# Windowed attention ahead of two feed-forward stages: 192 keys instead of 256 for each half of a query tile

## The chip, the cores and the metric

The program runs on one core of one Trainium2 chip. The metric is the device time of one execution in microseconds, taken as the median of several runs. The matrix engine TensorE is PE in the profile (its weight loads are PEld), VectorE is DVE, ScalarE is ACT, GpSimd is POOL, and SyncE is SP, which here issues all transfers between HBM and the on-chip memory SBUF. PE writes its results into PSUM, which is read by DVE and ACT alone.

## The reference

Two batches of 768 tokens pass through an attention of 8 heads of 64, in which a query sees the first n_global = 8 keys and the n_local = 96 latest keys, itself among them. Two feed-forward stages with squared ReLU follow. Inputs and results are float32.

```
scores = scale * q @ k.T
keep = is_global | (0 <= q_pos - k_pos < n_local)
scores = where(keep, scores - slope[h] * dist, -1e9)
a = exp(scores - max(scores)); a = a / (sum(a) + 1e-9)
x = a @ v                                       # (1536, 512)
x = (s * relu(x @ w_in)**2 + b) @ w_out         # 512 -> 2048 -> 512
out = relu(x @ w_in2)**2 @ w_out2
```

## The kernel before

The 1536 tokens make 12 query tiles of 128: tile n is block n // 2 of batch n % 2. Tiles 0 and 1 meet only their own 128 keys. Each of the other ten meets 256 keys in two blocks: its own 128, and the 32 first keys of the sequence with the last 96 of the block before it. The host lays these keys and values side by side, so one transfer per tile brings q and both blocks of k, and another brings both blocks of v (`load`).

The attention of a tile goes in these steps, each a task of a planner:
- `qk`, for one half of the heads (four heads, two pairs): one float32 matmul for each head, 64 rows (a head's features) by 128 columns (the queries), with 256 keys streamed through. The two heads of a pair lie in the upper and the lower 64 partitions, and so in two halves of the array; they write two PSUM buffers. A float32 matmul is two passes in the trace, so a `qk` of four matmuls shows as x8.
- `ttr`, on DVE, adds the bias `ND` (one table for each head, written by `consts` and `slopes` at the start) to the scores, stores the sum in SBUF and takes its extreme. `exp`, on ACT, and `norm`, on any of DVE, ACT and POOL, make the probabilities from it, with `rsum` between them for the reciprocal of the sums.
- `tr`, for one pair of heads, transposes 128 x 512 probabilities by four PE transposes of 128x128 into a PSUM buffer, and `tput`, on ACT or DVE, copies these to SBUF.
- `pv`, for a tile: 16 matmuls, each 128 keys by 64 features of v as the weights with 128 queries streamed through; two heads of a pair write the two halves of the partitions, so two matmuls share the array side by side (x32 in the trace). Weights are loaded anew for every pass.
- `xhi` (ACT) and `xlo` (DVE) split the result into two parts X, which the feed-forward matmuls take.

All of this takes PSUM from one pool of four buffers, `psA`: two for a `qk`, one for a `tr`, one for a `pv`.

The feed-forward stages work in three reduced-precision products for each float32 one. The first four of 16 chunks of the first stage (`h`, line 743, and `y`, line 822, 12 matmuls each with 256 tokens streamed) are run between the attention's tiles; `h` of the first 256 tokens needs tiles 0 and 1 only. When the attention is over, `second` opens more buffers and the remaining chunks follow, by a Strassen-like scheme (line 589 and lines 686 and 692). Their weights come as 64-bit numbers, which DVE and ACT decode.

What stands where on each engine is set by `Plan.run`, a list scheduler that is run when the program is built. `order` gives it each task with engines and costs, a due time, buffers and predecessors; the tables `SHIFT` and `PIN` at line 69 move the due times of named tasks and fix the engine of others. Each engine then runs its own list strictly in that order and waits by semaphores. Until the first `h`, the scheduler fills idle PE time with matmuls on a block of zeros (`warm`, line 375), whose result nobody reads.

Of the kernel before, what the change touches and what calls it, by code (L numbers as in the profile page):

```python
# [8 lines left out]
F32 = mybir.dt.float32  # L9
F32R = mybir.dt.float32r  # L10
I32 = mybir.dt.int32
# [14 lines left out]
HALF = (slice(0, D), slice(D, P))  # L26
NF = 4
# [31 lines left out]
def decoded(a):  # L59
# [9 lines left out]
SHIFT = {('at', 2, 0): 33.9, ('at', 3, 3): -39, ('at', 6, 3): 19.8, ('at', 7, 1): 22.2, ('at', 7, 3): -16.6, ('at',  # L69
    9, 2): 47, ('cadd', 10, 1, 1, 0): -83.9, ('cadd', 14, 1, 1, 0): 138, ('cadd', 16, 0, 0, 1): -56, ('cadd', 18, 0,  # L70
    0, 1): 32.3, ('cadd', 24, 0, 1, 1): -68.8, ('cadd', 28, 0, 1, 1): -48.5, ('cadd', 4, 0, 0, 1): -48.7, ('cadd',
# [21 lines left out]
    1): -12.5, ('norm', 4, 1): 170.3, ('norm', 4, 2): 40.3, ('norm', 5, 0): -22.9, ('norm', 6, 1): -2.8, ('norm', 7,  # L93
# [7 lines left out]
    ('qk', 3, 1): -39.7, ('qk', 8, 1): -104.8, ('relu', 2, 1280): 46.4, ('relu', 2, 256): -80.8, ('relu', 20, 1, 0,  # L101
    1): -45.4, ('relu', 22, 1, 0, 1): 119.7, ('relu', 24, 1, 1, 0): 12.5, ('relu', 4, 0, 1, 0): 2.1, ('rs', 10, 0):
# [1302 lines left out]
```

## Time and profile before

| | before |
|---|---|
| median of 3 runs | 598.61 us (598.4 to 598.61) |
| the profiled execution | 598.59 us |
| its span, first to last instruction | 596.8 us |
| PE busy | 586.8 us, 98% |
| DVE busy | 504.8 us, 85% |
| ACT busy | 363.5 us, 61% |
| POOL busy | 107.4 us, 18% |
| HBM read and written | 51.4 MB, 86 GB/s over the span |

The profiled execution lies within 0.02 us of the median, and 1.8 us of it lie outside the span. Busy time of PE is the union of its matmuls, whose ends are modelled and overlap, so what a stretch of matmuls occupies is read from the start of one group to the start of the next. The profile's chain of what ended last is empty for this execution, so the argument goes by the stretches and by the waits.

### The profile page before, as it was taken

How to read it: one execution, taken by the hardware profiler on the slowest of the kernel's cores; microseconds unless marked ns; L12 is line 12 of the kernel's file. 1: busy time of each engine (PE TensorE's matmuls, PEld its weight loads, DVE VectorE, ACT ScalarE, POOL GpSimd, SP SyncE). 2: the span in 40 equal slices, each digit the busy share in tenths (PEclk: the TensorE clock that was granted, in tenths of full speed). 3: DMA queues.
4: the chain of work that ended last, by engine and by line, in shares of the span. 5: the costliest groups of instructions: out<-in, count | busy, mean ns of one | idle time of the engine just before them, and what ended most of it. 6: DMA issues, size and time to landing. Idle time of an engine off the chain costs nothing.

```text
span 596.8 us, 10149 instructions
## 1 busy us (share of the span) xinstructions
PE 586.8 (98%) x3684; PEld 530.5 (89%) x3684; DVE 504.8 (85%) x1133; ACT 363.5 (61%) x796; POOL 107.4 (18%) x179
## 2 busy tenths in 40 slices
PE   7999999999999999999999999999999999999995
PEld 5788888899999989999999999998898989999894
DVE  7898989799999898999989999899987977874542
ACT  6999987776775646656656664666545544444330
POOL 4443424301100210031000121221120111100000
PEclk8999999999999999999999999999999999999999
DMA  7875631031220332204120311313323122100113
GB/s 278 299 268 173 220 109 36 3 107 36 59 84 2 106 86 91 98 8 156 36 93 2 106 36 36 101 41 110 102 70 107 37 70 63 44 1 1 44 64 110
DMA packets 14889, 52.11 MB, mean 87 GB/s; under 512 B 1904, under 2 KB 2160, under 8 KB 14832
## 3 DMA queue, kind: packets, MB, share of 16 engines
q1 hardware_dynamic: 14832, 51.39, 26.0%
q8 instruction: 31, 0.51, 0.4%
q14 instruction: 26, 0.21, 0.1%
HBM read 48.24 MB, written 3.15 MB: 86 GB/s over the span
## 4 chain that ended last, share of the span: by engine, by line


## 5 line engine op out<-in xcount | busy, mean ns | idle before, releaser
L589 PE MATMUL h<-xh,u 128*128 128x384 f32 x448 | 131.0, 337 | 0.0
L692 PE MATMUL yy<-u,gh 128*128 128x512 f32 x360 | 112.0, 392 | 0.0
L589 PE MATMUL h<-th,u 128*128 128x384 f32 x336 | 99.8, 338 | 0.2 <-DVE u L610 0.2
L686 PE MATMUL yy<-gh,u 128*128 128x512 f32 (+1 forms) x384 | 98.7, 337 | 0.0
L589 PEld LDWEIGHTS h<-xh,u 128*128 128x128 f32 x448 | 82.4, 188 | 1.1
L692 PEld LDWEIGHTS yy<-u,gh 128*128 128x128 f32 x360 | 67.1, 188 | 11.7
L589 PE MATMUL h<-xl,u 128*128 128x384 f32 x224 | 75.4, 337 | 0.0
L686 PEld LDWEIGHTS yy<-gh,u 128*128 128x128 f32 x384 | 67.2, 189 | 7.7
L692 PE MATMUL yy<-u,gl 128*128 128x512 f32 x180 | 70.4, 391 | 0.0
L272 ACT ACTIVATE u<-st 128x512 fp32r<-128x512 f32 (+1 forms) x63 | 40.1, 639 | 44.5 <-DVE st L55 18.7
L686 PE MATMUL yy<-gl,u 128*128 128x512 f32 (+1 forms) x192 | 64.8, 338 | 0.0
L589 PEld LDWEIGHTS h<-th,u 128*128 128x128 f32 x336 | 62.0, 188 | 2.3 <-DVE u L610 1.1
L589 PE MATMUL h<-tl,u 128*128 128x384 f32 x168 | 56.5, 337 | 0.0
L272 ACT ACTIVATE st<-st 128x512 f32<-128x512 f32 x64 | 42.8, 678 | 9.8 <-DMA st<-in_moe_w_out_dram 5.7
L52 DVE SCALAR_TENSOR_TENSOR st<-st 128x512 int32<-128x512 int32 x64 | 45.2, 707 | 2.5
L426 ACT ACTIVATE sn<-sn,nm 128x256 f32<-128x256 f32 (+1 forms) x96 | 46.2, 487 | 1.3 <-DVE nm L418 1.1
L55 DVE SCALAR_TENSOR_TENSOR st<-st 128x512 int32<-128x512 int32 x64 | 45.3, 711 | 1.1
L276 POOL TENSOR_SCALAR sn<-sn,rs 128x256 f32<-128x256 f32 (+1 forms) x68 | 34.8, 527 | 50.0 <-DVE rs L432 18.4
L589 PEld LDWEIGHTS h<-xl,u 128*128 128x128 f32 x224 | 42.1, 188 | 1.0
L610 DVE TENSOR_TENSOR u<-h,m 128x384 f32<-128x384 f32 x56 | 30.9, 552 | 14.1 <-PE h L589 13.4
L276 POOL TENSOR_SCALAR u<-st 128x512 fp32r<-128x512 f32 (+1 forms) x29 | 20.6, 712 | 111.6 <-DVE st L55 42.7
L692 PEld LDWEIGHTS yy<-u,gl 128*128 128x128 f32 x180 | 33.8, 188 | 7.5
(146 smaller groups left out, 1224.6 us busy)
## 6 DMA issues: line engine op xcount, KB each, us to landing
st<-in_moe_w_in_dram SPq DMA_DIRECT2D x32, 512.0 KB, 4.3
st<-in_moe_w_out_dram SPq DMA_DIRECT2D x32, 512.0 KB, 3.6
q<-in_qk_dram SPq DMA_DIRECT2D x10, 768.0 KB, 6.1
v<-in_v_dram SPq DMA_DIRECT2D x10, 512.0 KB, 4.8
out_dram<-acc SPq DMA_DIRECT2D x11, 256.0 KB, 2.2
q<-in_qk_dram SPq DMA_DIRECT2D x2, 512.0 KB, 5.6
v<-in_v_dram SPq DMA_DIRECT2D x2, 256.0 KB, 6.7
out_dram<-acc SPq DMA_DIRECT2D x2, 128.0 KB, 3.2
```

Of the source, the lines that this page charges most:

```text
L52: nc.vector.scalar_tensor_tensor(out=lo, in0=hi, scalar=3, in1=lo, op0=ALU.logical_shift_left, op1=ALU.bitwise_or)
L55: nc.vector.scalar_tensor_tensor(out=lo, in0=hi, scalar=-(1 << 31), in1=lo, op0=ALU.bitwise_and, op1=ALU.bitwise_or)
L272: nc.scalar.activation(out=out, in_=in_, func=AF.Copy, scale=scale)
L276: nc.gpsimd.tensor_scalar(out=out, in0=in_, scalar1=scale, scalar2=0.0, op0=ALU.mult, op1=ALU.add)
L426: self.nc.scalar.activation(out=sn[:, x], in_=sn[:, x], func=AF.Exp, scale=-1.0, bias=self.nm[:, n, h:h + 1], accum_out=self.rs[:, n, h:h ...
L589: self.nc.tensor.matmul(ps, p, q, start=first and kt == 0 and x == 0, stop=kt == 1 and x == 2, skip_group_check=not first)
L610: self.nc.vector.tensor_tensor(out=t, in0=self.T["h", a, tp, 1], in1=self.T["m1", a, tp], op=ALU.add)
L686: self.nc.tensor.matmul(yj, p[:, js], q[:, lo:hi], start=first and x == 0 and not (side and j % 2), stop=last and x == 2 and not (side and ...
L692: self.nc.tensor.matmul(y[m], p[:, ms], q, start=first and x == 0, stop=last and x == 2)
```

## The change

For the ten tiles with two key blocks, the 128 queries are taken in two halves of 64, and each half meets 192 keys: a query is at most 96 keys behind its block's start, so the first half needs the far 96, the first 32 and the first 64 of its own, the second half the last 32 of the far ones, the first 32 and all 128 of its own. The parts:

1. `qk`: eight matmuls of 64 rows by 64 columns with 192 keys streamed, where four of 64 by 128 with 256 stood. The four of a head pair lie in the four 64x64 pieces of the array. Score buffer u holds one head for the first 64 queries and the other head for the second 64 (heads swapped between halves); the two matmuls that share an output half write different buffers.
2. `ttr`, `exp`, `norm` and `tput` work on 192 or 384 elements instead of 256 or 512. The bias tables have 192 columns and swap heads too: `consts` has two more iotas on POOL and five more instructions on DVE, and `slopes` scales by a column of exponents instead of a constant.
3. `tr`: three transposes for a pair instead of four.
4. `pv`: 16 matmuls with all 128 rows and 64 streamed queries, and then 16 of 64 rows by 64 columns with 64 streamed, in four pieces of the array. It takes two PSUM buffers instead of one, and `xhi` and `xlo` run twice, on half of the columns each.
5. The layout on the host follows; the transfers keep their sizes.
6. The planner's costs follow, and `SHIFT` and `PIN` are other tables throughout. The fallback `general`, which runs only for other parameters, is adapted.

```diff
+W = P + D
-SHIFT = {('at', 2, 0): 33.9, ('at', 3, 3): -39, ('at', 6, 3): 19.8, ('at', 7, 1): 22.2, ('at', 7, 3): -16.6, ('at',
+SHIFT = {('at', 2, 2): 28.4, ('at', 2, 3): 26.5, ('at', 3, 0): 33, ('at', 3, 1): 42, ('at', 4, 1): -16.3, ('at', 5,
...
+QK, PV = 0.78, 1.55
...
-        self.ND = at.tile([P, H, 2 * P], BF16, name="ND")
+        self.ND = at.tile([P, H, W], BF16, name="ND")
...
+            m, n = P - G - D, P - G
+            nc.vector.tensor_scalar(out=self.sl.bitcast(I32), in0=self.sl.bitcast(I32), scalar1=23, scalar2=None,
+                                    op0=ALU.logical_shift_left)
+            nc.vector.tensor_scalar(out=far[:, 1, 0:n], in0=nr[:, 1, 0:n], scalar1=self.nl, scalar2=-NEG, op0=ALU.is_ge,
                                     op1=ALU.mult)
-            nc.vector.tensor_tensor(out=dist[:, 1, :], in0=dist[:, 1, :], in1=far[:, 1, :], op=ALU.min)
-            nc.vector.tensor_copy(dist[:, 1, 0:G], key[:, 1, 0:G])
+            b = self.band
+            nc.vector.tensor_tensor(out=b[:, D:D + m], in0=dist[:, 1, D:n], in1=far[:, 1, D:n], op=ALU.min)
+            nc.vector.tensor_copy(b[:, P - G:P], key[:, 1, 0:G])
+            nc.vector.tensor_copy(b[:, P:W], dist[:, 0, 0:D])
...
-            copy_r(self.nc, e, self.ND[:, h], self.dist.rearrange("p a t -> p (a t)"), 2.0 ** (2 - h))
+            copy_r(self.nc, e, self.ND[:, h], self.band[:, (1 - h % 2) * D:(1 - h % 2) * D + W], self.sl[:, h:h + 1])
...
     def qk(self, n, hf):
...
-        for x, hp in enumerate(hps):
-            for e in range(2):
-                self.nc.tensor.matmul(s[e][:, x], q[HALF[e], hp, :], k[HALF[e], a, hp], start=True, stop=True)
-                self.T["s", n, 2 * hp + e] = s[e][:, x].rearrange("p a t -> p (a t)")
...
+        s = [self.psa()[:, 0:2 * W].rearrange("p (x t) -> p x t", x=2) for _ in range(2)]
+        for x, hp in enumerate(range(2 * hf, 2 * hf + 2)):
+            for u in range(2):
+                self.T["s", n, 2 * hp + u] = s[u][:, x]
+            for u in range(2):
+                for e in range(2):
+                    t = HALF[u ^ e]
+                    mm(s[u][t, x], q[HALF[e], hp, t], k[HALF[e], hp, (1 - u) * D:(1 - u) * D + W], start=True, stop=True)
...
     def tr(self, n, g):
...
+        tr(t[:, 0:2 * W].rearrange("p (a b) -> p a b", a=2)[:, :, 0:D], sn[:, 0:P], self.ident)
+        tr(t[:, 2 * P:3 * P], sn[:, P:2 * P], self.ident)
+        tr(t[:, D:D + P], sn[:, 2 * P:3 * P], self.ident)
...
     def pv(self, n):
...
+        o = [self.psa()[:, 0:2 * P].rearrange("p (x t) -> p x t", x=4) for _ in range(2)]
+        for y in range(2):
+            self.T["o", n, y] = o[y]
+        for rest in range(2):
+            for hp in range(4):
+                for side in range(2):
+                    for e in range(2):
+                        h, r = 2 * hp + e, e ^ side
+                        if rest:
+                            mm(o[side][HALF[e], hp], v[HALF[r], 1, h * D:(h + 1) * D],
+                               at(hp)[HALF[r], 2 * P + side * D:2 * P + side * D + D], start=False, stop=True,
+                               skip_group_check=True)
+                        else:
+                            mm(o[side][HALF[e], hp], v[:, 0, h * D:(h + 1) * D],
+                               at(hp)[:, side * P + e * D:side * P + e * D + D], start=hp == 0, stop=False,
+                               skip_group_check=True)
...
-                add(("qk",) + u, {"PE": 0.97 if two else 1.1}, lambda e, u=u: f.qk(*u), dq, t, acq=[("a", "s", x) + u for x in range(2)],
+                add(("qk",) + u, {"PE": QK if two else 1.1}, lambda e, u=u: f.qk(*u), dq, t, acq=[("a", "s", x) + u for x in range(2)],
...
+            t - 3, acq=[("a", "o", n, y) for y in range(1 + two)], rel=[("at", n, g) for g in grp(n, None)] + [("v", n)])
```

Three places of the built program show how the lists move. The first is PE at the second `qk` of tile 3 and the `pv` of tile 2, between two `h` of the first chunks (a: a PSUM buffer; q, at, v: tiles of those steps; x4: four alike in a row). Before:

```order
L743 MATMUL h_0_510<-xh,u_83 128x256
L410 MATMUL a<-q_225 128x256 x4
L464 MATMUL a<-at_0_466,v_184 64x128 x4
L464 MATMUL a<-at_1_445,v_184 64x128 x4
L464 MATMUL a<-at_2_508,v_184 64x128 x4
L464 MATMUL a<-at_3_524,v_184 64x128 x4
L743 MATMUL h_0_582<-xh,u_86 128x256
```

The `pv` follows the `qk` directly, and a `h` follows it. The same place now:

```order
L791 MATMUL h_0_527<-xh,u_83 128x256
L435 MATMUL a<-q_237 64x192 x8
L509 MATMUL a<-at_0_499,v_205 64x64 x4
L509 MATMUL a<-at_1_474,v_205 64x64 x4
L509 MATMUL a<-at_2_558,v_205 64x64 x4
L509 MATMUL a<-at_3_546,v_205 64x64 x4
L505 MATMUL a<-at_0_499,v_205 64x64 x4
L505 MATMUL a<-at_1_474,v_205 64x64 x4
L505 MATMUL a<-at_2_558,v_205 64x64 x4
L505 MATMUL a<-at_3_546,v_205 64x64 x4
L791 MATMUL h_0_611<-xh,u_86 128x256
```

The place in the list is the same; line 509 is the part with all rows and line 505 the part in four pieces. In both programs three `qk` and four sets of transposes of the ten large tiles stand ahead of the first `h`, and 17 and 36 behind it.

The second place is DVE at the start (acc: room that the constants borrow; nv: the two window sizes; ND: bias tables; sg, rt, tmp: constants of the first feed-forward stage, made from sb). Before:

```order
L352 TENSOR_TENSOR acc<-acc 128x128
L274 TENSOR_SCALAR ND_142<-acc 128x128 x3
L354 TENSOR_SCALAR acc<-acc,nv 128x128
L356 TENSOR_TENSOR acc<-acc 128x128
L357 COPY acc<-acc 128x32
L762 TENSOR_SCALAR sg<-sb 128x1
L763 TENSOR_SCALAR sg<-sg 128x1
L764 TENSOR_TENSOR tmp<-sb,sg 128x1
L765 TENSOR_TENSOR sgb<-sb,sg 128x1
L766 TENSOR_SCALAR rt<-tmp 128x1
L768 TENSOR_SCALAR rt<-rt 128x1
L418 ISA sn_0_228,nm<-a,ND_142 128x128
```

Now the constants of sb and one step of the root (nine instructions) stand ahead of the bias tables:

```order
L1408 SCALAR_TENSOR_TENSOR nv<-nf 128x2
L810 TENSOR_SCALAR sg<-sb 128x1
L811 TENSOR_SCALAR sg<-sg 128x1
L812 TENSOR_TENSOR tmp<-sb,sg 128x1
L813 TENSOR_TENSOR sgb<-sb,sg 128x1
L814 TENSOR_SCALAR rt<-tmp 128x1
L816 TENSOR_SCALAR rt<-rt 128x1
L819 RECIPROCAL tmp<-rt 128x1
L820 SCALAR_TENSOR_TENSOR rt<-tmp,rt 128x1
L821 TENSOR_SCALAR rt<-rt 128x1
L352 TENSOR_SCALAR acc<-acc,nv 128x128
L354 TENSOR_SCALAR acc<-acc,nv 128x128
```

Behind the first bias table come the eight instructions of the other one, and the first `ttr` of tile 0 stands behind all of them:

```order
L275 TENSOR_SCALAR ND_142<-acc 128x128
L360 TENSOR_SCALAR acc<-acc 128x8
L362 TENSOR_SCALAR acc<-acc,nv 128x96
L365 TENSOR_TENSOR acc<-acc 128x32
L366 COPY acc<-acc 128x32
L367 COPY acc<-acc 128x64
L368 TENSOR_TENSOR acc<-acc 64x64
L369 COPY acc<-acc 64x64
L370 COPY acc<-acc 128x64
L275 TENSOR_SCALAR ND<-acc 128x192
L275 TENSOR_SCALAR ND_142<-acc 128x128
L443 ISA sn_0_241,nm<-a,ND_142 128x128
```

The third place is the head of SP's list, which issues the transfers. Before:

```order
L1340 DMA ni<-in_n_dram 128x4
L394 DMA q_163<-in_qk_dram 128x1024
L1351 DMA sb<-in_sb_dram 128x2
L37 DMA st_0_166<-in_moe_w_in_dram 128x1024
L397 DMA v_168<-in_v_dram 128x512
```

Now the small transfer of sb has passed the first q:

```order
L1400 DMA ni<-in_n_dram 128x4
L1411 DMA sb<-in_sb_dram 128x2
L409 DMA q_166<-in_qk_dram 128x1024
L38 DMA st_0_168<-in_moe_w_in_dram 128x1024
L412 DMA v_170<-in_v_dram 128x512
```

The first q is issued one transfer later than before; number and sizes of the transfers are as they were.

## Rows read from the trace of the kernel before

**Rows 1.** The page, busy time of the engines and share of the span.

```profile
PE 586.8 (98%) x3684; PEld 530.5 (89%) x3684; DVE 504.8 (85%) x1133; ACT 363.5 (61%) x796; POOL 107.4 (18%) x179
```

**Rows 2.** Busy time in five stretches, all engines; columns in the first line.

```profile
core 0: us, PE busy (x) PEld busy (x) DVE busy (x) ACT busy (x) POOL busy (x), PEclk, DMA share, GB/s
0.00:26.40 26.40, 22.69 (x179) 15.62 (x180) 20.59 (x107) 21.38 (x74) 12.69 (x38) 0.94 0.84 316
26.40:118.00 91.60, 91.60 (x893) 80.32 (x893) 81.05 (x274) 80.64 (x239) 33.26 (x59) 1.00 0.41 134
118.00:200.00 82.00, 82.00 (x568) 79.02 (x565) 78.60 (x152) 54.40 (x103) 8.05 (x12) 1.00 0.17 52
200.00:575.00 375.00, 374.78 (x1986) 342.76 (x1985) 318.47 (x592) 204.97 (x379) 53.36 (x70) 1.00 0.21 68
575.00:596.80 21.80, 15.72 (x71) 12.77 (x69) 6.09 (x11) 2.08 (x4) 0.00 (x0) 0.95 0.21 76
```

**Rows 3.** Waits of PE, whole span: for whom, us in total, times, longest.

```profile
PE a L410 <- DMA q<-in_qk_dram: 2.1, 2, 1.9
...
PE h L589 <- DVE u L610: 0.2, 1, 0.2
PE a L443 <- POOL sn L276: 0.2, 1, 0.2
```

**Rows 4.** Timeline of PE, 13.9 to 26.7 us: start, us, what.

```profile
14.80 1.14 PE L410 MATMUL a<-q 64*128 64x256 f32 x8
...
17.10 1.09 PE L464 MATMUL a<-at,v 128*64 128x128 f32 x16
18.13 0.66 PE L443 MATMUL a<-ident,sn 128*128 128x128 f32 x4
18.71 1.13 PE L410 MATMUL a<-q 64*128 64x256 f32 x8
...
20.47 1.06 PE L443 MATMUL a<-ident,sn 128*128 128x128 f32 x8
...
21.74 0.63 PE L443 MATMUL a<-ident,sn 128*128 128x128 f32 x4
...
23.32 1.14 PE L410 MATMUL a<-q 64*128 64x256 f32 x8
...
25.33 1.33 PE L443 MATMUL a<-ident,sn 128*128 128x128 f32 x8 [0.22 <-POOL sn L276]
26.41 0.36 PE L743 MATMUL h<-xh,u 128*128 128x256 f32 x1
```

**Rows 5.** Timeline of PE, 47 to 51 us.

```profile
47.72 1.13 PE L410 MATMUL a<-q 64*128 64x256 f32 x8
48.78 1.97 PE L464 MATMUL a<-at,v 128*64 128x128 f32 x32
50.68 0.39 PE L743 MATMUL h<-xh,u 128*128 128x256 f32 x1
```

**Rows 6.** Groups of DVE by line and shape: busy us, mean ns, idle before.

```profile
L418 DVE CUSTOM_DVE_ANT_0 sn<-a,ND 128x256 f32<-128x256 f32 x80 | 29.6, 418 | 4.6 <-PE a L410 3.9 <-POOL sn L276 0.4
...
L473 DVE TENSOR_TENSOR xl<-a,xh 128x512 fp32r<-128x512 f32 x12 | 8.2, 684 | 0.8 <-ACT xh L469 0.5
...
L418 DVE CUSTOM_DVE_ANT_0 sn<-a,ND 128x128 f32<-128x128 f32 x16 | 3.6, 282 | 0.0
```

**Rows 7.** Timeline of DVE, the start.

```profile
6.94 0.15 DVE L762 TENSOR_SCALAR sg<-sb 128x1 f32<-128x1 f32 x1
...
7.84 0.29 DVE L418 CUSTOM_DVE_ANT_0 sn<-a,ND 128x128 f32<-128x128 f32 x1
```

**Rows 8.** Timeline of ACT, the start.

```profile
9.46 0.39 ACT L426 ACTIVATE sn<-sn,nm 128x128 f32<-128x128 f32 x1
...
24.27 0.61 ACT L469 CAST xh<-a 128x512 fp32r<-128x512 f32 x1
```

More of the change, by code (lines that the diff above doesn't have):

```diff
@@ L441, in tr @@
         t = self.T["t", n, g] = self.psa()
-        for x in range(4):
-            self.nc.tensor.transpose(t[:, x * P:(x + 1) * P], sn.rearrange("p h k -> p (h k)")[:, x * P:(x + 1) * P],
-                                     self.ident)
+        tr = self.nc.tensor.transpose
+        if n < 2:
+            for x in range(4):
+                tr(t[:, x * P:(x + 1) * P], sn[:, x], self.ident)
+            return
+        sn = sn.rearrange("p h k -> p (h k)")
+        tr(t[:, 0:2 * W].rearrange("p (a b) -> p a b", a=2)[:, :, 0:D], sn[:, 0:P], self.ident)
@@ L450, in tput @@
         else:
-            self.nc.vector.tensor_copy(at, self.T.pop(("t", n, g)))
+            self.nc.vector.tensor_copy(at, self.T.pop(("t", n, g))[:, 0:w])
     def pv(self, n):
-        blk = self.blocks(n)
-        nb = blk.stop - blk.start
-        o = self.T["o", n] = self.psa().rearrange("p (x t) -> p x t", x=4)
-        v = self.T["v", n]
-        for hp in range(4):
-            for a in range(blk.start, blk.stop):
+        v, mm = self.T["v", n], self.nc.tensor.matmul
+        at = lambda hp: self.T["at", n, hp // 2 if n < 2 else hp]
@@ L460, in pv @@
+        if n < 2:
+            o = self.T["o", n, 0] = self.psa().rearrange("p (x t) -> p x t", x=4)
+            for hp in range(4):
                 for e in range(2):
                     h = 2 * hp + e
-                    hs = self.heads(n, hp // 2 if n < 2 else hp)
-                    c = ((h - hs[0]) * nb + a - blk.start) * P
-                    self.nc.tensor.matmul(o[HALF[e], hp, :], v[:, a, h * D:(h + 1) * D],
-                                          self.T["at", n, hp // 2 if n < 2 else hp][:, c:c + P],
-                                          start=(a == blk.start), stop=(a == blk.stop - 1))
@@ L468, in xhi @@
-    def xhi(self, n):
-        self.nc.scalar.copy(out=self.X[0][:, :, n * P:(n + 1) * P], in_=self.T["o", n])
-    def xlo(self, n):
-        xh, xl = (x[:, :, n * P:(n + 1) * P] for x in self.X)
-        self.nc.vector.tensor_tensor(out=xl, in0=self.T.pop(("o", n)), in1=xh.bitcast(F32), op=ALU.subtract)
+                    mm(o[HALF[e], hp, :], v[:, 0, h * D:(h + 1) * D], at(hp)[:, h % 4 * P:h % 4 * P + P], start=True,
+                       stop=True)
+            return
+        o = [self.psa()[:, 0:2 * P].rearrange("p (x t) -> p x t", x=4) for _ in range(2)]
@@ new lines, in pv @@
+        for y in range(2):
+            self.T["o", n, y] = o[y]
+        for rest in range(2):
+            for hp in range(4):
+                for side in range(2):
+                    for e in range(2):
+                        h, r = 2 * hp + e, e ^ side
[7 more added lines that the diff above has]
+                               skip_group_check=True)
@@ L476, in wload, with xcols, xhi, xlo @@
+    def xcols(self, n, y):
+        return [x[:, :, n * P:(n + 1) * P] if n < 2 else x[:, :, n * P + y * D:n * P + y * D + D] for x in self.X]
+    def xhi(self, n, y):
+        self.nc.scalar.copy(out=self.xcols(n, y)[0], in_=self.T["o", n, y])
+    def xlo(self, n, y):
+        xh, xl = self.xcols(n, y)
+        self.nc.vector.tensor_tensor(out=xl, in0=self.T.pop(("o", n, y)), in1=xh.bitcast(F32), op=ALU.subtract)
     def wload(self, w, i):
@@ L877, in order @@
     add("n", "SP:1.2", lambda e: None, key=-1000.0, dma=0.06)
[L878 removed]
+    add("nd0", "POOL:2.4", lambda e: f.consts(0), key=-60.0)
     add("nd1", "DVX:1.25", lambda e: f.consts(1), ["nd0", "n"], key=-60.0)
[L880 removed]
+    add("nd2", "DVX:1.1", lambda e: f.consts(2), ["nd1"], key=vt[2, 0] + cfg["att"] - 8)
     for h in range(H):
@@ L883, in order @@
             key=vt[0, h // 4] - 10)
-        add(("ndh", 1, h), "POOL:0.5 ACT:0.36 DVX:0.32", lambda e, h=h: f.slopes(False, h, e), ["nd2"],
+        add(("ndh", 1, h), "POOL:0.42 ACT:0.3 DVX:0.26", lambda e, h=h: f.slopes(False, h, e), ["nd2"],
             key=vt[2, h // 4] + cfg["att"] - 4)
@@ L907, in order @@
                 last = hf == 1 if not two else x == 1
-                add(("ttr",) + w, "DVE:0.7" if two else "DVE:0.85", lambda e, w=w: f.ttr(*w),
+                add(("ttr",) + w, "DVE:0.57" if two else "DVE:0.85", lambda e, w=w: f.ttr(*w),
                     [("qk",) + su] + [("ndh", int(two), h) for h in (range(2 * g, 2 * g + 2) if two else range(4 * g, 4 * g + 4))] +
@@ L911, in order @@
                     acq=[("sN",) + w], rel=[("a", "s", x) + su for x in range(2)] * last)
-                add(("exp",) + w, "ACT:0.99" if two else "ACT:1.55", lambda e, w=w: f.exp(*w), [("ttr",) + w], t - 1)
-                add(("norm",) + w, "DVX:1.0 ACT:0.82 POOL:1.0" if two else "DVX:1.0 ACT:1.2 POOL:1.45",
+                add(("exp",) + w, "ACT:0.84" if two else "ACT:1.55", lambda e, w=w: f.exp(*w), [("ttr",) + w], t - 1)
+                add(("norm",) + w, "DVX:0.85 ACT:0.7 POOL:0.8" if two else "DVX:1.0 ACT:1.2 POOL:1.45",
                     lambda e, w=w: f.norm(*w, e), [("rs",) + u], t - 1)
-                add(("tr",) + w, {"PE": 0.438}, lambda e, w=w: f.tr(*w), [("norm",) + w], t - 2,
+                add(("tr",) + w, {"PE": 0.33 if two else 0.438}, lambda e, w=w: f.tr(*w), [("norm",) + w], t - 2,
                     acq=[("a", "t") + w], rel=[("sN",) + w])
-                add(("at",) + w, "ACT:0.48 DVE:0.6", lambda e, w=w: f.tput(*w, e),
+                add(("at",) + w, "ACT:0.4 DVE:0.48" if two else "ACT:0.48 DVE:0.6", lambda e, w=w: f.tput(*w, e),
                     [("tr",) + w], t - 2, acq=[("at",) + w], rel=[("a", "t") + w])
@@ L920, in order @@
         t = vt[n, 1] + (cfg["att"] if two else -500.0)
-        add(("pv", n), {"PE": 1.8 if two else 1.0}, lambda e, n=n: f.pv(n), [("at", n, g) for g in grp(n, None)] + [("lv", n)],
-            t - 3, acq=[("a", "o", n)], rel=[("at", n, g) for g in grp(n, None)] + [("v", n)])
-        add(("xh", n), "ACT:0.52", lambda e, n=n: f.xhi(n), [("pv", n)], t - 3)
-        add(("xl", n), "DVE:0.6", lambda e, n=n: f.xlo(n), [("xh", n)], t - 3, rel=[("a", "o", n)])
-    xdone = lambda n: [("xl", n)]
+        add(("pv", n), {"PE": PV if two else 1.0}, lambda e, n=n: f.pv(n), [("at", n, g) for g in grp(n, None)] + [("lv", n)],
+            t - 3, acq=[("a", "o", n, y) for y in range(1 + two)], rel=[("at", n, g) for g in grp(n, None)] + [("v", n)])
+        for y in range(1 + two):
+            add(("xh", n, y), "ACT:0.31" if two else "ACT:0.52", lambda e, n=n, y=y: f.xhi(n, y), [("pv", n)], t - 3)
+            add(("xl", n, y), "DVE:0.36" if two else "DVE:0.6", lambda e, n=n, y=y: f.xlo(n, y), [("xh", n, y)], t - 3,
+                rel=[("a", "o", n, y)])
+    xdone = lambda n: [("xl", n, y) for y in range(1 if n < 2 else 2)]
     for x in range(5):
```

145 lines of the change are left out of this document (88 added, 57 removed), and 114 rows, old and new, of tables (PIN, SHIFT).

## The prediction

> **What bounds the kernel now.** I read the page first, then the stretches, then who PE waits for, and last PE's timeline. The page gives PE 98% of the span and DVE 85% [rows 1]. The stretches show when: from 26.4 us, where the first `h` starts, to 575 us PE is busy all of the time but 0.2 us, at a granted clock of 1.00 (its upper level, 2.4 GHz) [rows 2]. In 26.4 to 118 us, where the attention lies, DVE and ACT are close behind (81.05 and 80.64 of 91.6 us), and behind it, up to 200 us, DVE has 78.60 of 82 us. PE waits for DVE or POOL twice, for 0.2 us each; the wait for q, 2.1 us, is at the start [rows 3]. So a microsecond of array time that goes after 26.4 us should come off the end, as long as the others keep up. Before 26.4 us it is worth nothing by itself: what PE doesn't need there is filled with idle matmuls.
>
> **Prices on PE.** A group's place is from its start to the next group's start. A `pv` of 32 matmuls takes 50.68 - 48.78 = 1.90 us [rows 5]; a small one of 16 takes 18.13 - 17.10 = 1.03 us, and their busy times differ by 1.97 - 1.09 = 0.88 us [rows 4, 5]. These are 8 more side-by-side pairs with 128 queries streamed: 0.110 us a pair, 0.86 ns a column. 16 pairs are 1.76, so 0.14 us of 1.90 are the first weight load and the change to another split of the array. A `qk` takes 48.78 - 47.72 = 1.06 us [rows 5]: 4 pairs of 256 columns at 0.86 ns are 0.88, and 0.18 are fixed. Four more transposes add 1.06 - 0.63 = 0.43 us [rows 4], 0.108 us each.
>
> **The change, part by part.**
>
> - `qk`: 16 passes of 192 columns. If the four pieces of the array work at once, these are 4 groups of 192 x 0.86 = 0.165 us, 0.66 us. To that I add 0.14, the fixed part of `pv`, whose first weights have 64 columns too: 0.80 us, 0.26 less than now. With 0.18 it would be 0.22 less. 17 of the 20 lie behind the first `h` (three are in rows 4, ahead of it): -4.4 us.
> - `pv`: 16 pairs of 64 columns at 0.055 us are 0.88; then 8 groups of four at 0.055 are 0.44; and two fixed parts of 0.14, since the split of the array changes in the middle: 1.60 us instead of 1.90. Ten times: -3.0 us. No row has passes this short; the bounds are the rivals below.
> - `tr`: one transpose less, 0.108 us, in 36 of 40 sets behind the first `h`: -3.9 us. The waits are unchanged.
> - The rest of the attention is beside PE. `ttr` at 192 columns should take about 350 ns, halfway between 282 at 128 and 418 at 256 [rows 6]; 80 of them, -5.4 us on DVE. `xlo` runs twice on half the columns; with the fixed part that the two `ttr` rows give, 282 - 136 = 146 ns, this is 0.146 us more for each of ten tiles, +1.5 us. `exp`, `norm` and `tput` get shorter in the same way. I count none of this: it is what lets DVE and ACT follow.
> - The start. Nine small instructions now precede the bias tables on DVE, and five new ones follow. Six of the nine stood ahead of the first `ttr` before too, at 7.84 - 6.94 = 0.90 us [rows 7], 0.15 each; so three more are 0.45 us, and the five, at 0.15 to 0.29 (the `ttr` of 128 columns in the same rows), 0.75 to 1.45. The first `ttr`, now at 7.84 us, could start 1.2 to 1.9 us later. But its reader, `exp` on ACT, starts only at 9.46 us [rows 8], and from there to `xhi` of tile 1 at 24.27 us it is ACT's list, busy 21.38 of the first 26.4 us [rows 2], that gets shorter. Bounds 0 to +1.9 us, and I take +0.5, nearer to the cover. SP issues q one transfer later; the same free time covers it, and all sizes are the same.
> - New waits. `pv` now takes two of the four PSUM buffers, so the `qk` or `tr` next in PE's list can wait until `xhi` and `xlo` have read one. And all lists are in another order. The waits after the start are 0.4 us now [rows 3], and nothing bounds them above but the third rival. I take +0.5.
>
> Sum: -4.4 - 3.0 - 3.9 + 0.5 + 0.5 = -10.3 us. The profiled execution is 598.59 us, of which 596.8 are the span, and it is equal to the median of 598.61: **588.3 us**.
>
> **Rivals.**
>
> First, **the pieces work two by two** (slower). The rows show two heads in two row halves that write two PSUM buffers (`qk`), and two column halves that write one buffer (`pv`) [rows 5]. None shows all four at once, nor two row halves writing the same buffer, which is what the new `qk` does in score buffer u and the new `pv` in each of its two. If only two can go on, `qk` is 8 x 0.165 + 0.14 = 1.46 us, 17 x 0.40 = +6.8; `pv` is 0.88 + 0.88 + 0.28 = 2.04 us, +1.4; with -3.9 and +1.0 this is +5.3: 603.9 us. It decides from the point where a group of four takes 1.66 times its 0.165 us (10.3 of the 15.6 us between the cases). What speaks for four: each of the two splits alone runs two at once in the rows, and no two matmuls in the air share both a buffer and an output half. The Trainium skill, "TensorEngine Tiling (Array Packing)", Restrictions and Gotchas, speaks against the change: different row tiles cannot access the same PSUM bank at once. By that rule the first rival holds, if its bank is meant whole; no row of this kernel has such a case, so I give the rival 11 in 100.
>
> Second, **weight loads come out from under the short passes** (slower). Each pass loads its own weights. Four transposes with 128-column loads go at 0.108 us, so 64 columns need about 0.055 us, just what a pass of 64 queries streams. If load and stream don't overlap, a group of `pv` is 0.11 us: 16 + 8 groups are 2.64, with 0.28 it is 2.92 us, +10.2 for ten; `qk` streams 0.165 us over a load of 0.055 and keeps its -4.4; with -3.9 and +1.0 this is +2.9: 601.5 us. Against it: weight loads are busy 80.32 us of the 91.6 us in which PE is busy all the time [rows 2], so they run under matmuls, and the pairs of `pv` now cost no more than a transpose of as many columns. The Trainium skill, "TensorE: Matmul & The Clock Gate", Part 3, has loads overlapping with matmuls in flight only where the row groups differ. By that rule the first 16 pairs of `pv`, which use all rows, would lose the overlap; the rows just named speak against it. 6 in 100.
>
> Third, **DVE becomes the bound** (faster, but less). DVE has 81.05 us of work in 26.4 to 118 us; less 5.4 and plus 1.5 it is 77.2. The forecast wants it in 91.6 - 11.3 = 80.3 us, a share of 96%. If it can't pass its present 88.5%, the stretch takes 87.2 us, 4.4 less than now, and with +0.5 at the start the time is 594.7 us. The four PSUM buffers would show in the same way. Against it: in 118 to 200 us DVE has a share of 96% [rows 2] with PE never waiting. 15 in 100.
>
> **How the numbers follow.** The forecast has 64 in 100, with a range of its own from 585.5 (all 20 `qk` and 40 `tr` count, no new wait, a little off the fixed parts) to 592. A mixture, groups of four at about 1.6 times their pace, that ends where it began has 4; the rivals have 11, 6 and 15. A measurement of this kernel can tell about 0.2%, 1.2 us. Faster: the forecast and the third rival, 0.79. Same: the mixture, 0.04. Slower: the first and the second, 0.17. The range of 8 in 10 is 585.5 to 600: it takes in the third rival and the mixture and leaves out the two slower cases.
>
> **What would show it.** Right: `qk` groups of 16 passes at 0.8 us and `pv` of 64 passes at 1.6 us, start to start; PE without gaps from the first `h`, which stays at about 26 us; the last `pv` some 10 us earlier than now. The first rival: `qk` at 1.46 us, passes of one group starting in two steps. The second: `pv` near 2.9 us, `qk` at 0.8. The third: the right prices on PE, but waits of some 5 us for DVE or ACT in the attention. The forecast would be wrong altogether if PE's lists behind the attention began to wait, which no part of the change touches but the order.

## The result and the profile after

The changed kernel takes 591.9 us, median of four runs (591.19 to 592.58), against 598.53 of before beside it: ratio 0.9889, 95% interval 0.9872 to 0.9906. That is 6.6 us less; 10.3 were forecast. The profiled execution is the slowest of the four, 592.58 us, with a span of 590.5 us. In a second measurement, the base of the experiments below, the same kernel took 590.92 us (590.23 to 591.66), ratio 0.9875 [0.986, 0.989], 7.6 us less than before.

PE is busy for 576.9 us of this span, again 98%, and DVE for 83%. The stretches up to 567 us (start and end of each; its length; busy time, with the instructions in brackets, of PE, PEld, DVE, ACT and POOL; granted clock; DMA share and rate), and whom PE waits for, of the changed kernel:

```profile
0.00:28.20 28.20, 22.80 (x201) 15.02 (x201) 20.47 (x115) 19.55 (x70) 13.70 (x43) 0.94 0.75 289
28.20:110.30 82.10, 82.08 (x1272) 72.64 (x1271) 72.24 (x275) 75.40 (x256) 32.92 (x61) 1.00 0.46 153
110.30:192.00 81.70, 81.26 (x599) 77.09 (x598) 76.38 (x148) 53.74 (x105) 6.65 (x10) 1.00 0.16 52
192.00:567.00 375.00, 375.00 (x1992) 343.62 (x1991) 317.08 (x594) 209.03 (x387) 41.96 (x62) 1.00 0.21 68
```

```profile
PE a L470 <- POOL sn L277: 2.2, 1, 2.2
PE a L425 <- DMA q<-in_qk_dram: 1.8, 2, 1.3
PE warm L386 <- DVE idle L383: 1.3, 1, 1.3
PE yy L734 <- DVE gl L711: 0.3, 1, 0.3
```

Beside [rows 1, 2, 3]: from the first `h` on PE is still busy nearly all of the time at a clock of 1.00, and waits once, 0.3 us. So what was taken from PE there did come off the end. DVE has 88% of the stretch with the attention, ACT 92%; neither holds PE up. The first `h`, however, starts at 28.17 us instead of 26.41. PE's last output matmul of the kernel before, and the first `h` and the last output matmul of the changed kernel's second profile:

```profile
590.33 0.40 PE L701 MATMUL yy<-u,gl 128*128 128x512 f32 x1
```

```profile
28.25 0.36 PE L791 MATMUL h<-xh,u 128*128 128x256 f32 x1
...
582.27 0.40 PE L749 MATMUL yy<-u,gl 128*128 128x512 f32 x1
```

From the first `h` to the last output matmul it is 590.33 - 26.41 = 563.9 us before and 582.27 - 28.25 = 554.0 now, 9.9 less (9.7 in the first profile, whose last output matmul starts at 582.40).

PE's timeline in the middle of the attention (start, duration from the first start to the last end, line, tiles, passes), beside [rows 4, 5]:

```profile
46.04 0.88 PE L435 MATMUL a<-q 64*64 64x192 f32 x16
46.85 0.39 PE L791 MATMUL h<-xh,u 128*128 128x256 f32 x1
...
48.47 1.15 PE L509 MATMUL a<-at,v 128*64 128x64 f32 x32
49.55 0.69 PE L505 MATMUL a<-at,v 64*64 64x64 f32 x32
50.18 0.33 PE L473 MATMUL a<-ident,sn 128*128 128x128 f32 x1
50.35 0.27 PE L474 MATMUL a<-ident,sn 128*128 128x128 f32 x1
50.46 0.27 PE L475 MATMUL a<-ident,sn 128*128 128x128 f32 x1
```

Start to start, a `qk` takes 46.85 - 46.04 = 0.81 us, a `pv` 50.18 - 48.47 = 1.71 us, and transposes in a row still 0.11 us each, of which there are three in a set (lines 473 to 475).

The start, on DVE and on ACT (in brackets the idle time before a row and what ended it), beside [rows 7, 8]:

```profile
6.21 0.15 DVE L810 TENSOR_SCALAR sg<-sb 128x1 f32<-128x1 f32 x1 [2.26 <-DMA sb<-in_sb_dram]
...
7.68 0.28 DVE L352 TENSOR_SCALAR acc<-acc,nv 128x128 f32<-128x128 f32 x1
```

```profile
11.81 0.38 ACT L451 ACTIVATE sn<-sn,nm 128x128 f32<-128x128 f32 x1
```

`root(0)` now stands ahead of the bias tables on DVE and waits 2.26 us for `sb`, a transfer of two numbers. With root's 1.47 us behind it the first table starts at 7.68 us, the first `ttr` at 11.10 instead of 7.84, and the first `exp` at 11.81 instead of 9.46.

### The profile page after: what moved, and what is told of

It is laid out like the page before. It is cut to its first block, busy times and chain, and to the rows that moved or that the text cites. A ratio compares the mean times of both kernels' runs of the same rounds, so it can differ in the third digit from the quotient of the medians.

```text
span 590.5 us, 11060 instructions
## 1 busy us (share of the span) xinstructions
PE 576.9 (98%) x4125; PEld 521.2 (88%) x4125; DVE 492.3 (83%) x1139; ACT 359.9 (61%) x820; POOL 95.2 (16%) x176
## 4 chain that ended last, share of the span: by engine, by line
## 5 line engine op out<-in xcount | busy, mean ns | idle before, releaser
L273 ACT ACTIVATE u<-st 128x512 fp32r<-128x512 f32 (+1 forms) x58 | 36.5, 635 | 38.5 <-DVE st L56 25.5
L277 POOL TENSOR_SCALAR u<-st 128x512 fp32r<-128x512 f32 (+1 forms) x34 | 25.9, 764 | 172.0 <-PE h L637 62.2
L53 DVE SCALAR_TENSOR_TENSOR st<-st 128x512 int32<-128x512 int32 x64 | 44.6, 698 | 3.3
L56 DVE SCALAR_TENSOR_TENSOR st<-st 128x512 int32<-128x512 int32 x64 | 44.3, 693 | 1.0
L451 ACT ACTIVATE sn<-sn,nm 128x192 f32<-128x192 f32 (+1 forms) x96 | 41.7, 441 | 0.2 <-DVE nm L443 0.2
L671 DVE TENSOR_TENSOR u<-h,u 128x384 f32<-128x384 f32 x56 | 30.9, 552 | 11.1 <-PE h L637 10.6
```

Source lines behind the costliest of these rows:

```text
L53: nc.vector.scalar_tensor_tensor(out=lo, in0=hi, scalar=3, in1=lo, op0=ALU.logical_shift_left, op1=ALU.bitwise_or)
L56: nc.vector.scalar_tensor_tensor(out=lo, in0=hi, scalar=-(1 << 31), in1=lo, op0=ALU.bitwise_and, op1=ALU.bitwise_or)
L273: nc.scalar.activation(out=out, in_=in_, func=AF.Copy, scale=scale)
L277: nc.gpsimd.tensor_scalar(out=out, in0=in_, scalar1=scale, scalar2=0.0, op0=ALU.mult, op1=ALU.add)
L451: self.nc.scalar.activation(out=sn[:, x], in_=sn[:, x], func=AF.Exp, scale=-1.0, bias=self.nm[:, n, h:h + 1], accum_out=self.rs[:, n, h:h ...
L671: self.nc.vector.tensor_tensor(out=self.T["r", a, tp, c, side], in0=self.T["h", a, tp, bank], in1=m, op=ALU.add)
```

## The experiments

All times below are medians, to be read against 590.92 us of the unaltered kernel; the experiments were run in three sets, each on another chip, and the kernel before took 598.47 to 598.71 us in them.

### The price of the passes

**Other order of the passes in `qk`**

```diff
                 self.T["s", n, 2 * hp + u] = s[u][:, x]
-            for u in range(2):
+        for u in range(2):
+            for x, hp in enumerate(range(2 * hf, 2 * hf + 2)):
                 for e in range(2):
                     t = HALF[u ^ e]
...
```

> The sixteen passes of a qk in another order: first the eight for score buffer 0, which lie in the two diagonal pieces of the array, then the eight for buffer 1 in the other two; the same work, but only two pieces have something to do at a time. Theory (four pieces at once is what makes qk 0.81 us): eight groups of two at 0.165 us and 0.14, 1.46 us a qk, 17 of them behind the first h, +11 us, about 602 us; passes start in pairs about 160 ns apart. Two row halves then write one buffer at the same time; if they can't, a pass stands alone, 16 x 0.16 = 2.6 us a qk and +31 us. Rival (the time of a qk is set by its weight loads or its issue, 16 at 0.05 us): qk stays at 0.8 us and the time at 591.

Measured: 591.34 us (590.98 to 591.91). PE's timeline of this kernel, one `qk` and what follows:

```profile
45.78 0.89 PE L436 MATMUL a<-q 64*64 64x192 f32 x16
46.61 0.39 PE L792 MATMUL h<-xh,u 128*128 128x256 f32 x1
```

A `qk` takes 0.83 us, which is the rival's number. But it can be had in another way: if the passes for buffer 1 start while those for buffer 0 still wait for their pieces, four are at work again, and the edit did not do what it was made for. The time alone doesn't tell these apart; the next run puts the passes where only two pieces can work.

**All passes in two pieces**

```diff
-                    mm(s[u][t, x], q[HALF[e], hp, t], ...)
+                    mm(s[u][HALF[e], x], q[HALF[e], hp, t], ...)
```

> All sixteen passes of a qk go to the two diagonal pieces of the array: each head writes its scores for both query halves to its own output half, so the heads are not swapped between halves and the result is another one; the sizes, the number of passes and all that follows are the same. Theory (qk is 0.81 us because four pieces work at once, whatever the order they are fed in): now eight groups of two, 8 x 0.162 and 0.15, 1.45 us a qk, +0.63 us, 17 times, +10.8 us, about 602 us. Rival (a qk is set by the loads of its weights or the issue of its passes, 0.04 us each): 0.81 us a qk and 591 us.

Measured: 602.88 us (602.79 to 602.97). Again one `qk`, and this kernel's first `h`:

```profile
45.88 1.52 PE L435 MATMUL a<-q 64*64 64x192 f32 x16
47.33 0.39 PE L791 MATMUL h<-xh,u 128*128 128x256 f32 x1
```

```profile
29.70 0.36 PE L791 MATMUL h<-xh,u 128*128 128x256 f32 x1
```

A `qk` takes 1.45 us, 0.64 more, as the theory had it. 17 x 0.64 = 10.9 us, and the first `h` is 1.5 us later than the changed kernel's 28.17; together 12.4, measured 12.0. So four pieces do work at once, and this is worth 0.64 us a `qk`. The number of passes of that line in the first 0.16 us of a `qk` (in brackets; then the clock, DMA share and rate) shows it too, for the changed kernel, the other order and the two pieces, in this sequence:

```profile
46.04:46.20 0.16, 0.16 (x4) 1.00 0.28 103
```

```profile
45.78:45.94 0.16, 0.16 (x4) 1.00 0.38 154
```

```profile
45.88:46.04 0.16, 0.16 (x2) 1.00 0.59 205
```

In the other order, too, four passes begin at once, although eight for one diagonal stand first in the list: the edit did not leave two pieces idle, and its 0.83 us say nothing for the rival. The run on two pieces shows a second thing: both row halves here write the same score buffer (in its two output halves) and still go two at a time; one after the other, 16 passes would have taken 2.6 us.

**`pv` with its two kinds in turns**

```diff
-        for rest in range(2):
-            for hp in range(4):
+        for hp in range(4):
+            for rest in range(2):
```

> pv takes its two kinds of passes in turns, for each head pair first those with all 128 rows and then those of 64: seven changes between the two splits of the array instead of one; the same passes, so the same result. Theory (the fixed part of about 0.3 us a pv is two changes of split, 0.09 to 0.15 us each): six more changes are 0.5 to 0.9 us, pv 2.25 to 2.6 us instead of 1.71, ten times, +5 to +9 us, 596 to 600 us. Rival (the fixed part is the first weight load alone, and the pace of 58 ns a group is all the rest): pv stays within 0.1 us of 1.71, the time within 1 us of 591.

Measured: 600.06 us (599.37 to 601.39), +9.1. One `pv` on PE:

```profile
50.16 0.45 PE L509 MATMUL a<-at,v 128*64 128x64 f32 x8
50.54 0.34 PE L505 MATMUL a<-at,v 64*64 64x64 f32 x8
50.81 0.45 PE L509 MATMUL a<-at,v 128*64 128x64 f32 x8
...
52.78 0.33 PE L473 MATMUL a<-ident,sn 128*128 128x128 f32 x1
```

52.78 - 50.16 = 2.62 us, 0.91 more for six more changes: 0.15 us each, and ten times 0.91 is the 9.1 measured. The rows give the pace too. 16 pairs of the first kind take 49.55 - 48.47 = 1.08 us, four take 0.38: 0.058 us a pair, 0.15 fixed. Eight groups of the second kind take 0.63 us, two take 0.27: 0.06 a group, 0.15 fixed. So 1.71 us are about 24 x 0.058 and two changes of 0.15. In turns the passes of 64 rows also add to what the passes just ahead of them have written; but the 0.15 is there in the unaltered order as well, where they don't, so this is not what costs it.

### The start

**root behind the first ttr**

```diff
+        if step < 2 and self.hold:
+            self.held.append(step)
+            return
...
+        if (n, g) == (0, 1):
+            self.hold = False
+            for step in self.held:
+                self.root(step)
```

(the first part in `root`, the second at the end of `ttr`)

> The nine small instructions for root(0) and root(1) stand behind the first tile's ttr on DVE instead of ahead of the bias tables; all else, SP's order too, is unaltered. Theory: what made the start late is DVE's wait of 2.26 us for sb in front of them, together with their 1.47 us; then the first bias table starts at about 4.0 us instead of 7.68, exp no later than 9.6 instead of 11.81, the first h at 26.2 to 26.9 instead of 28.17, and the time falls by 1.3 to 2.0 us against the unaltered kernel. Rival: the start is held by q (qk of tile 0 ran at 7.51 us) or by what ACT and POOL do behind it; then the first h stays within 0.5 us of 28.17 and the time within 0.5 us.

Measured: 589.36 us (589.1 to 589.73), 1.56 less, with no overlap of the runs; ratio to before 0.9849 [0.9835, 0.9862]. The `ttr`, and PE's first `h`:

```profile
8.84 0.29 DVE L443 CUSTOM_DVE_ANT_0 sn<-a,ND 128x128 f32<-128x128 f32 x1 [1.29 <-PE a L425]
```

```profile
26.94 0.37 PE L795 MATMUL h<-xh,u 128*128 128x256 f32 x1
```

The first bias table starts at 4.06 us, the first `exp` at 9.38, and the first `h` comes 1.2 to 1.3 us earlier than in the two profiles of the unaltered kernel (28.17 and 28.25). The theory holds, but the list on DVE is not all of the 1.56 us. Some 0.35 us of them lie outside the span: time less span is about 2.1 us in all eight runs of the unaltered kernel and about 1.75 in these five; no row shows why.

Another part is PE's clock. In the changed kernel PE had waited 2.2 us for the first normed probabilities, and then worked at the lower level (1.2 GHz). The run with three copies at the end of the program (below) has the same start and the same wait of 2.2 us, but there the clock stayed up. The stretch from 16 to 18 us, first of the changed kernel, then of that run (the clock is the third number from the end), and the first `h` of that run:

```profile
16.00:18.00 2.00, 2.00 (x16) 1.21 (x20) 1.95 (x13) 2.00 (x10) 1.95 (x5) 0.50 1.06 437
```

```profile
16.00:18.00 2.00, 1.98 (x23) 1.20 (x23) 1.97 (x13) 2.00 (x11) 1.94 (x5) 1.00 1.06 437
```

```profile
27.78 0.37 PE L795 MATMUL h<-xh,u 128*128 128x256 f32 x1
```

So the lower clock costs the first `h` 0.4 us here (0.6 against the latest such profile, 28.42 us in the run with one copy). With root late PE waited 1.4 us and stayed at 1.00; in the run with root late and idle matmuls at the end it fell, and the first `h` came at 27.39 us. At like clocks, 27.78 against 26.94 and 28.17 to 28.42 against 27.39, root late is worth 0.8 to 1.0 us. How much of that is the wait for `sb` and how much the nine instructions' own 1.47 us, no run separates.

**root further back, and sb behind q**

```diff
+        if step < 2 and not self.late:
+            return
+        if step == 2:
+            self.late = True
+            for x in range(2):
+                self.root(x)
```

> root(0) and root(1) moved further back on DVE than in the run with root late, directly ahead of root(2), behind the attention's first rsum. There the nine instructions (1.47 us) stood between the first ttr and the rsum that norm on POOL waited for, and PE waited 1.4 us for that norm. Theory (this list on DVE still sets the start): the first norm starts 1.2 to 1.8 us earlier than 13.67 us, the first h at 25.4 to 26.4 instead of 26.94, the time 588.0 to 588.9. Rival (ACT's list of exps, 9.38 to 25 us, binds): the first h at 26.7 to 27.2, the time 589.2 to 589.6.

Measured: 589.4 us (588.58 to 590.64); ratio 0.9844 [0.9832, 0.9857]. The first norm came at 12.18 us, 1.5 earlier, and PE's first transposes at 12.88 instead of 14.37, but the first `h` of the profiled execution only at 27.98. That execution is the slowest of the five. Two things show in its rows. The first is the rsum of the first large tile and the norm that needs it, and PE's transposes behind that; first with root late, then here:

```profile
20.87 0.18 DVE L461 RECIPROCAL rs<-rs 128x4 f32<-128x4 f32 x1
21.24 1.64 POOL L277 TENSOR_SCALAR sn<-sn,rs 128x192 f32<-128x192 f32 x4 [0.67 <-ACT at L485]
22.41 0.30 PE L477 MATMUL a<-ident,sn 128*128 128x128 f32 x1
```

```profile
21.27 0.18 DVE L457 RECIPROCAL rs<-rs 128x4 f32<-128x4 f32 x1
21.64 1.63 POOL L277 TENSOR_SCALAR sn<-sn,rs 128x192 f32<-128x192 f32 x4 [2.60 <-ACT at L481]
22.18 0.30 PE L473 MATMUL a<-ident,sn 128*128 128x128 f32 x1 [1.39 <-POOL sn L277]
```

The nine instructions, moved out of the way of the first norm, now stand in the way of this one (they start at 17.38 us), so its rsum comes 0.4 us later than before the move and PE has only 0.23 of its 1.5 us left. The profile names a copy on ACT as what the norm waited for; but the norm starts 0.19 us behind the end of DVE's reciprocal in both executions and 0.20 in the next kernel, while it starts 0.18, 0.00 and 0.03 us behind the end of that copy. So DVE's list holds it, and not ACT's. The second thing is the clock:

```profile
23.57 1.97 PE L493 MATMUL a<-at,v 128*64 128x128 f32 x16
25.48 0.47 PE L473 MATMUL a<-ident,sn 128*128 128x128 f32 x1
```

```profile
24.00:26.00 2.00, 2.00 (x19) 0.52 0.15 61
```

After the wait of 1.39 us the clock fell, and a `pv` of tile 0 or 1, 1.03 us in [rows 4], took 25.48 - 23.57 = 1.91. The median lies in the rival's range and two of the five runs, 588.58 and 589.08 us, at or near the theory's. The list on DVE did set the start, further down too, and so the move took back most of what it gave; the clock took more in the profiled execution.

Loading `sb` behind q of tile 1 was tried first with root late:

```diff
             start(out=t[:, a], in_=self.qk_[b, i, :, a])
+            if n == 1:
+                self.load_sb()
...
-    add("sb", "SP:0.47", lambda e: f.load_sb(), key=-895.0, dma=0.06)
+    add("sb", "SP:0.47", lambda e: None, key=-895.0, dma=0.06)
```

> root(0) and root(1) late as in the earlier run, and sb loaded behind q of tile 1 instead of ahead of q of tile 0. Theory (with root out of the way the start hangs on q: DVE waited 1.29 us for qk of tile 0, and PE 0.72 us for q): q lands 0.4 to 0.5 us earlier, the first exp and the first h come 0.3 to 0.5 us earlier than with root late alone (9.38 and 26.94 us), and the time is 588.9 to 589.1 us. Rival (norm on POOL, ACT's list or the weights of the first decode bind behind it): the first h stays at 26.9 and the time at 589.4.

Measured: 589.45 us (589.11 to 590.54), no gain. The q came through (the first `exp` at 8.52 us), but DVE waited for `sb` once more, ahead of what the first norm needs:

```profile
10.30 0.15 DVE L819 TENSOR_SCALAR sg<-sb 128x1 f32<-128x1 f32 x1 [0.69 <-DMA sb<-in_sb_dram]
```

The first norm came only 0.2 us earlier (13.45 against 13.67), PE waited 2.8 us for it, and its clock fell (0.50 from 16 to 18 us); the first `h` came 0.4 us later.

Then both edits together, with root ahead of root(2):

> The same with sb loaded behind q of tile 1. With root late that brought the first exp from 9.38 to 8.52 us but the first h from 26.94 to 27.37, since DVE then waited 0.69 us for sb behind the ttr. Theory (with root far behind, sb is no longer waited for, and the earlier q comes through): the first h 0.4 to 0.9 us earlier than in the run without the move, the time 587.3 to 588.4. Rival (another wait takes its place, by ACT's list or POOL's norms): no difference from that run within 0.3 us.

Measured: 588.54 us (587.57 to 588.85), ratio 0.9824 [0.9811, 0.9836]: 0.9 less than without the move and 2.4 less than the changed kernel, the fastest of all. PE's first transposes of the first large tile and its first `h`:

```profile
21.46 0.30 PE L475 MATMUL a<-ident,sn 128*128 128x128 f32 x1 [1.40 <-POOL sn L277]
...
25.77 0.36 PE L793 MATMUL h<-xh,u 128*128 128x256 f32 x1
```

Between these two profiles the move gives 0.7 us, 21.46 against 22.18. The other 1.5 us between their first `h`, 25.77 against 27.98, go with the clock: the lists behind that point are the same, and here it stayed at 1.00 behind a wait as long.

### The end

In the profiled execution of the change, SP's last two issues took 2.35 us, where they take 0.81 in the kernel before. SP's own rows of that execution, of the kernel before, and of the unaltered kernel's second profile:

```profile
583.28 2.35 SPq L777 DMA_DIRECT2D out_dram<-acc  x2
```

```profile
591.22 0.81 SPq L729 DMA_DIRECT2D out_dram<-acc  x2
```

```profile
583.16 0.82 SPq L777 DMA_DIRECT2D out_dram<-acc  x2
```

The span ends 4.7 to 4.9 us behind the last issue in all three (590.5, 596.8 and 588.7 us), so the long issue is 1.5 us of that execution's time. An instruction fetch began at about the same moment, which gave a theory.

> The changed kernel once more, unaltered, as the base for the others on the same chip. By the theory that the end of the program is a race (the last output transfer's issue on SP took 1.93 us in the profile of the change and 0.38 us in that of before, while a 16 KB instruction fetch began 0.1 us behind it), its runs fall on two levels about 1.3 to 1.5 us apart, near 591.2 and 592.5 us, and a run with a short issue has a span near 589. By the rival, that the issue is always this long in the changed kernel, they lie on one level near 592.

Measured: 590.92 us; 590.23, 590.84, 591.0 and 591.66: one band, not two levels. The profile has the short issue and, as expected for it, a span near 589.

```diff
+        if m == 5:
+            w = self.psH.tile([P, 512], F32, tag="h", name="idle_end")
+            for _ in range(4):
+                self.nc.tensor.matmul(w, oh[:, 0:P], oh, start=True, stop=True)
```

> Four matmuls of 128x512 whose result nobody reads, 0.22 us each, stand on PE behind the last output matmul; nothing waits for them. Theory: the instruction fetch near the end follows PE's last instructions (1.4 us behind the start of its last matmul in the profile of the change, 1.6 us in that of before), so it comes 0.9 us later, when SP has issued the last transfer; that issue takes 0.4 us in every run, the time from the last output matmul's start to the end of the span falls from 8.04 to 6.5 us, and the runs lie at 590.8 to 591.3 us on one level. Rival: the fetch has nothing to do with it; then the issue stays at 1.9 us, and the time at 592 or above.

> Both edits together: root(0) and root(1) late, and four idle matmuls at the end. If both theories hold they add, 1.3 to 2.0 us from the start and up to 1.5 us from the end: 589 to 590 us. If the start theory alone holds, about 590.3; if the end theory alone, about 591.2; if neither, 592.

Measured: 590.62 us (590.35 to 591.0) with the idle matmuls alone, 589.74 (589.15 to 590.31) with root late too, which without them took 589.36. The issues were short, but they were in the unaltered kernel also. So no gain can be told. The opposite was tried, to push the last issue onto the fetch:

```diff
+            if cols.start == 256:
+                r = self.rp.tile([P, SB], F32, tag="r", name="idle_dve")
+                nc.vector.tensor_copy(r[:, 0:256], self.acc[:, 0:256])
             nc.vector.tensor_tensor(out=a, in0=self.T["y", tp][j][:, cols], in1=a, op=ALU.add)
```

> A copy of 128x256 on DVE, read by nobody, stands ahead of the last addition of the output, so SP issues the last transfer 0.3 to 0.5 us later; PE's end stays where it is. Theory (the issue is stretched when it falls on the instruction fetch that follows PE's end): the issue now falls behind the start of the fetch, takes 1 to 2 us instead of 0.4, and the time is 1.2 to 2 us above the unaltered kernel's 590.9 on its chip. Rival (the long issue was chance and has no tie to the fetch): the issue stays at 0.4 us and the time rises by the copy alone, 0.3 to 0.5 us.

> Three copies of 128x256 on DVE instead of one ahead of the last addition of the output; one put the last transfer's issue 0.34 us ahead of the fetch, with no effect. Two more put it 0.4 us later, 1.9 us behind the start of PE's last matmul, where the fetch has begun (1.4 to 1.8 us behind it in the profiles so far). Theory (an issue that falls on the fetch lasts until 0.3 to 0.4 us behind the fetch's end): an issue of 1 to 1.6 us, a tail from the last matmul's start to the end of the span of 7.6 to 8.4 us, and a time 1.3 to 2 us above the unaltered kernel's 590.9. Rival (no tie): an issue of 0.4 us, a tail of 7.0 us, and 0.6 us above.

Measured: 590.54 us (589.99 to 590.93) with one copy, 591.12 (590.53 to 591.88) with three. From the last output matmul to the end of the span it is 6.5 and 7.1 us, as the rival had it for three (6.4 in the unaltered kernel's second profile). The last issue with three copies, and the instruction queue's row from 583.40 us to the issue (packets, MB, its whole time as a share of that stretch on 16 engines):

```profile
583.73 0.33 SPq L777 DMA_DIRECT2D out_dram<-acc  x1
```

```profile
q8 instruction: 1, 0.02, 30.0%
```

The fetch was under way, and the issue took 0.33 us. The theory, by which it would have lasted until the fetch's end, falls. What made one issue long in one of the profiles is open, and so is how many of the first four runs had it.

## Why the prediction was right and wrong

The sign and the range were right (591.9 in 585.5 to 600), the likeliest time 3.6 us too low. The number alone decides little: 591.9 is nearer to the third rival's 594.7 than to 588.3, and it is the rows that rule this rival out. Step by step, against the working on record:

- **`qk`, -4.4 us: right.** 0.81 us measured for 0.80, so 17 x 0.25 = -4.3. The first rival falls: its price of 1.46 us is right (1.45 when only two pieces have work), its condition isn't met. The Trainium skill, "TensorEngine Tiling (Array Packing)", Restrictions and Gotchas, says that different row tiles cannot access the same PSUM bank at once; the run on two pieces differs: there two row halves write one buffer (2 KB of each partition, taken to be one bank), each its own output half, and go at once at 0.162 us a group.
- **`pv`, -3.0 us: mis-sized.** 1.71 us, not 1.60: 24 x 0.058 and two fixed parts of 0.15, where the forecast had 0.055 and 0.14. Ten times 0.19 is -1.9 us, so 1.1 of the missing 3.6. The mechanism was right, down to the second change of split. The second rival falls: at 0.058 us a pair the loads are under the passes. By the rule of "TensorE: Matmul & The Clock Gate", Part 3, of the Trainium skill, that loads overlap only where row groups differ, a pair would have taken 0.11 by the prediction's estimate; the trace does not agree. The same part also has loads into a background weight buffer pulled ahead, which would fit; no run here shows such a buffer.
- **`tr`, -3.9 us: right.** Three transposes at 0.11 us, 36 sets.
- **The rest beside PE, nothing: right.** A `ttr` takes 0.35 us as forecast, DVE has 72.24 us of 82.1, and the third rival's waits aren't there.
- **New waits, +0.5 us: too much, by 0.2 to 0.3.** The 0.4 us of the kernel before were misread: one of the two waits, at 25.33 us in [rows 4], lies ahead of the first `h`. Behind it PE was idle for 0.2 us in the kernel before and is for 0.5 now.
- **The start, +0.5 us: the step that failed.** The first `h` came 1.8 us later and did not stay at about 26 us. The step counted the nine instructions that move ahead of the tables, but not what the first of them waits for: `sb`, 2.26 us on DVE. So the first `ttr` came 3.26 us later, where 1.2 to 1.9 were reckoned, and the first `exp` 2.35; that the first `h` stayed within the bound of +1.9 is luck. With root behind the `ttr` 0.8 to 1.0 us of it come back. Nor did "the same free time covers it" hold for q: the `qk` of tile 0 starts at 7.51 us instead of 5.57, with root late DVE waits 1.29 us for it, and `sb` behind q brings 0.7 us once root is out of the way. The clock, which fell in the wait for the late probabilities, was not in the step either: 0.4 to 0.6 us.
- **The end and the time outside the span, not in the sum.** The first profiled execution has 1.5 us for one long issue; in the second profile it isn't there. Outside the span lie 2.1 us instead of 1.8, in all eight runs.

With these the sum closes. The prices, less 0.3 us for the waits, give 4.3 + 1.9 + 3.9 - 0.3 = 9.8 us behind the first `h`; the profiles have 9.9 and 9.7. Less 1.8 for the start and 0.3 outside the span, the second profile's 9.9 are 7.8: it took 590.84 us, 7.75 less than the profiled 598.59. Less 1.6 more behind the last output matmul the first profile's 9.7 are 6.0: it took 592.58 us. Why the two medians, 591.9 and 590.92 us, lie 1.0 apart is thereby shown for one execution of each alone.

One sign was badly chosen: the last `pv` was to come 10 us earlier. It starts at 113.06 us instead of 116.83, presumably since the lists put the `h` and `y` between the tiles in another order; this was not followed. Where the work goes is read from the prices and the end, not from the place of a task that a planner may move.

## What to carry to other kernels

When a list is reordered, look not only at how long the moved instructions are but at what the first of them waits for, and write down when that lands; on DVE's list a transfer of two numbers cost more here (2.26 us) than the nine instructions behind it (1.47). Instructions that are moved out of one reader's way can end in the next one's, so compare the same row further down, and not only the first. Cost short passes as a pace and a fixed part for each change of the array's split, and test "side by side" by putting the work where it can't be, since a changed order alone may leave it as it was. Where a profile names what ended a wait, compare the distance to it over several executions. A wait of PE at the start can be paid twice, once as the wait and again at the lower clock behind it.

## What the runs showed of the hardware that was not expected

- The order in which passes for four pieces stand in PE's list did not matter within a `qk` of sixteen: eight for one diagonal and then eight for the other took 0.83 us, against 0.81 in turns and 1.45 when only one diagonal had work. Four passes began within the first 0.16 us in either order, and one diagonal runs only two at a time, so passes began ahead of others that stand before them in the list.
- A change between the split of the array in two column halves and in four pieces costs 0.15 us in either direction.
- The clock after a wait at the start is not the same in each execution, even of the same start: behind a wait of 2.2 us it fell to the lower level in six profiles and stayed at 1.00 in one; behind 1.39 us it fell in one kernel, and behind 1.40 us it stayed in its neighbour. This moved the first `h` by 0.4 to 1.5 us. What decides it is open.
- The time outside the span is about 2.1 us in every run of the changed kernel and of four of its variants, and 1.7 to 2.0 us in every run of the others, with the same results to write. What decides it is open.
- A small transfer can be slow to land: `sb`, 1 KB, was issued at 1.25 us and landed 4.9 us later, and behind q and other transfers it took 7.1.
